# The last feed-forward's second product in seven block products for tile pairs, with its weights' conversions two at a time in the expert slots

## The chip, the cores and the metric

One core of one Trainium2 chip runs the kernel. The metric is device microseconds of one execution. The core's engines work side by side, each through its own queue in order: TensorE (PE; its weight loads are listed apart as PEld), VectorE (DVE), ScalarE (ACT), GpSimd (POOL) and SyncE (SP), which here only issues transfers.

## The reference

Attention over 4 batches, 8 heads, 576 positions of 64 gives 2304 tokens of 512. A mixture of 8 experts (top 1, hidden size 1024) follows, and a dense feed-forward of hidden size 2048. Cut to the last two:

```python
def _moe_ref(x, expert_emb, tau, w1, w2):     # x 2304x512, w1 8x512x1024, w2 8x1024x512
    ...
    for e in range(E):
        mask = expert_idx == e
        h = np.maximum(x[mask] @ w1[e], 0.0)
        out[mask] = gate_w[mask, None] * (h @ w2[e])

def _moe2_ref(x, w_in, w_out):                # w_in 512x2048, w_out 2048x512
    h = x @ w_in
    r = np.maximum(h, 0.0)
    g = r * r
    return (g @ w_out).astype(np.float32)
```

## The kernel before

Every product is made of f16 parts: an operand is split in a high and a low f16 part, and three matmuls (high x high, high x low, low x high) stand for one. The order of the instructions on each engine is that of the code; waits between engines are put in by the program's buffers.

The kernel has three stages. Attention takes the first 395 us. Then come 22 expert slots of 128 tokens each (`run_slots`). Slot t gathers its tokens with indirect transfers on POOL (`gather_id`, `gather_x`), splits them (`x_split`: ACT the high part, POOL the low part), transposes them on PE (`x_T`), multiplies by the expert's first matrix (`ff1`, 2 x 48 matmuls of 128 columns, PSUM buffer `ph`) and by its second (`ff2`, 24 matmuls of 512 columns), and stores the rows in `y_d` (`ff2_out`): the early slots in order through SP, the later ones by an indirect scatter on POOL. The loop runs ahead: in slot t stand, in this order, `gather_x(t+4)`, `ff1(t+1, 0)`, `x_T(t+2)`, `x_split(t+3)`, `ff1(t+1, 1)`, `split_w1(t+2)` and `ff2(t)` with `ff2_out(t)`. `split_w1` splits a new expert's first matrix into the single buffer `w1b` (four times ACT and DVE), behind a branch that is taken only where the expert changes, which it does in eight slots.

The feed-forward's weights `win` and `wout` arrive as 64-bit floats and are made into two f16 parts by bit operations (`convert`): four on DVE, a copy with rounding on ACT (high part), a subtraction on DVE (low part). The 16 pieces of `win` and the first 4 of `wout`, each 512 columns wide, are converted in the slots, from slot 3 on (`piece`, `CPACE` 3.3 steps to a slot, three steps to a piece); the other 12 pieces of `wout` in the first two blocks of the last stage (`PACE2`). The slots' pieces of `wout` go to DRAM (`wosc`) and come back.

The last stage takes the tokens in five blocks, four of 4 tiles (512 columns) and one of 2 (256). `g_unit(j, f)` computes one of 16 slices of the hidden layer for block j: 12 matmuls with the weights stationary and the tokens moving, relu on ACT, the square on ACT (blocks 0 and 1) or DVE, and the split, which is put off by one unit (`g_split`: ACT high part, DVE low part). `o_unit(j, n)` computes the outputs of one tile with 48 matmuls of 512 columns:

```python
for f in range(16):
    for a, b in ((0, 0), (0, 1), (1, 0)):
        PE.matmul(p_, lhsT=g2[:, a, f, n * P:(n + 1) * P], rhs=woh[:, b, f, :],
                  start=(i == 0), stop=(i == 47))
```

Its result is scaled (ACT or DVE, by tile) and scattered to the output by POOL. The block's outputs stand between the next block's `g_unit`s, one for four of them, from block 2 on; those of block 0 follow block 1's units. The next block's tokens are loaded at f = 0 (`y_load`), split in units 4 to 10 (`y_split`) and transposed by a transfer.

Of the kernel before, what the change touches and what calls it, by code (L numbers as in the profile page):

```python
# [23 lines left out]
P = 128  # L24
# [59 lines left out]
def body(ctx: ExitStack, tc: tile.TileContext, q, k, v, wsm, emb, tau, mw1, mw2, win, wout, cst_d, lsk_d, ids_d, out):  # L84
# [9 lines left out]
    wosc = dram.tile([P, 2 * 16 * DM], F16, name="wosc")  # L94
# [856 lines left out]
    with tc.manual_schedule():  # L951
# [149 lines left out]
        def convert(i, wrp, bufs, woh=None):  # L1101
            wr = wrp.tile([P, 512, 2], U32, name="wr2", bufs=bufs)
            wf = wr.rearrange("p n t -> p (n t)")
            if i < 16:
                kc, n = divmod(i, 4)
                SP.dma_start(out=wf, in_=win[kc * P:(kc + 1) * P, n * 1024:(n + 1) * 1024])
                dh, dl = (wih[:, a, kc, n * 512:(n + 1) * 512] for a in range(2))
                s = WIS
            else:
                j = i - 16  # L1110
                SP.dma_start(out=wf, in_=wout[j * P:(j + 1) * P, :])
                if woh is None:
# [14 lines left out]
            DVE.scalar_tensor_tensor(out=b, in0=hi, scalar=0xC0000000, in1=b, op0=ALU.bitwise_and, op1=ALU.bitwise_or)  # L1127
            yield
            ACT.activation(dh, bf, AF.Copy, scale=s)
            yield  # L1130
            DVE.scalar_tensor_tensor(out=dl, in0=bf, scalar=s, in1=dh, op0=ALU.mult, op1=ALU.subtract)
            if i >= 16 and woh is None:
                SP.dma_start(out=wosc.rearrange("p (a n) -> p a n", a=2)[:, :, j * 512:(j + 1) * 512], in_=wo)


        def pieces(cs, ahead):
            for c in cs[:ahead]:
                next(c)
            yield
            for n, c in enumerate(cs):  # L1140
                next(c)
                yield
                next(c)
                yield
                if n > 0:
                    next(cs[n - 1], None)
                    if n - 1 + ahead < len(cs):
                        next(cs[n - 1 + ahead])
                next(c)
                yield  # L1150
            next(cs[-1], None)
            yield

# [65 lines left out]
        def ff2_out(t):  # L1219
            ys = ysp.tile([P, XW], F32, name="ys")  # L1220
            ACT.activation(ys[:, :DM], pys.pop(t), AF.Copy, scale=YS)
            POOL.tensor_copy(ys[:, DM:XW], ga.pop(t))
            if t < NEARLY:
                SP.dma_start(out=y_d[t * P:(t + 1) * P, :], in_=ys)
            else:
                POOL.indirect_dma_start(out=y_d, out_offset=bass.IndirectOffsetOnAxis(ap=yidx[:, t:t + 1], axis=0),
                                        in_=ys, in_offset=None, bounds_check=NT + P - 1, oob_is_err=False)
# [23 lines left out]
        def piece(t, n):  # L1251
            while t >= 3 and done[0] < (t - 3 + 0.25 * n) * CPACE:
                next(conv, None)
                done[0] += 1

        def run_slots(lo, hi):
# [34 lines left out]
            for t in range(lo, hi):  # L1291
# [56 lines left out]
        with ExitStack() as fctx:  # L1348
            fp = lambda n, bufs, **kw: tp(fctx, n, bufs, **(kw if "space" in kw else dict(side="right")))
            woh = fp("f_wo", 1).tile([P, 2, 16, DM], F16, name="woh")  # L1350
            gp = fp("f_g", 2)
            yrp = fp("f_yr", 1)
            wrp2 = fp("f_wr", 1)
            ytp = fp("f_yt", 1)
            rp2 = fp("f_r", 3)
            op_ = fp("f_o", 3)
            ysp2 = fp("f_ys", 2)
            pf1 = fp("f_p1", 4, space=PSUM)
            pf2 = fp("f_p2", 4, space=PSUM)
            blocks = [list(range(i, min(i + 4, NTILE))) for i in range(0, NTILE, 4)]  # L1360
            yts, gts, yrs, late = {0: y0}, {}, {}, []

            def y_load(j):
                n, i0 = len(blocks[j]), blocks[j][0]
                yrs[j] = yrp.tile([P, 4, XW], F32, name="yr")
                SP.dma_start(out=yrs[j][:, :n], in_=y_d[i0 * P:(i0 + n) * P, :].rearrange("(n p) c -> p n c", p=P))
                yts[j] = ytp.tile([P, 2, 4, 512], F16, name="y2") if j % 2 else y0

            def y_split(j, n):
                if n >= len(blocks[j]):  # L1370
                    return
                y2, yr = yts[j], yrs[j][:, n]
                y_rows(blocks[j][n], yr)
                ysr = ysp2.tile([P, 2, 4, P], F16, name="ysr")
                y4 = yr[:, :DM].rearrange("p (k n) -> p k n", k=4)
                ACT.copy(ysr[:, 0], y4)
                DVE.tensor_tensor(out=ysr[:, 1], in0=y4, in1=ysr[:, 0], op=ALU.subtract)
                SP.dma_start_transpose(out=y2.rearrange("p a k n -> p (a k) n")[:, :, n * P:(n + 1) * P],
                                       in_=ysr.rearrange("p a k n -> p (a k n)"))

            def g_unit(j, f):
                n = len(blocks[j]) * P
                y2 = yts[j]
                if f == 0:
                    gts[j] = gp.tile([P, 2, 16, 512], F16, name="g2")
                p_ = pf1.tile([P, 512], F32, name="pf1")
                i = 0
                for kc in range(4):
                    for a, b in ((0, 0), (0, 1), (1, 0)):
                        PE.matmul(p_[:, :n], lhsT=wih[:, a, kc, f * P:(f + 1) * P], rhs=y2[:, b, kc, :n],  # L1390
                                  start=(i == 0), stop=(i == 11))
                        i += 1
                r = rp2.tile([P, 512], F32, name="r")
                ACT.activation(r[:, :n], p_[:, :n], AF.Relu, scale=RS)  # L1394
                g = rp2.tile([P, 512], F32, name="g")
# [124 lines left out]
```

## Time and profile before

| | us |
|---|---|
| median of three runs | 1032.59 (1025.32 to 1034.40) |
| the profiled execution | 1032.91 |
| its span in the trace | 1031.1 |
| attention, to about | 395 |
| expert slots, to about | 643 |
| last feed-forward on PE | 643.16 to 1019.79 |

The span runs from the first instruction to the last, so 1.8 us of the profiled execution lie outside it. A timeline row gives start, duration, engine, line, operation, buffers and shape of neighbouring instructions that belong together, with their count, and in brackets the idle time ahead of the first and what ended it. Neighbouring groups of PE overlap by a matmul's run through the array, so the spacing of two starts tells what a group costs. A group's row gives busy time and the mean of one instruction in ns.

### The profile page before, as it was taken

The numbers are of one execution on the slowest core, as the hardware profiler recorded it, in microseconds if no ns is written. First come the engines' busy times: TensorE is split into PE (matmuls) and PEld (weight loads), VectorE is DVE, ScalarE is ACT, GpSimd is POOL, SyncE is SP. The second block draws the span as 40 slices with busy tenths as digits, with TensorE's granted clock in tenths as the row PEclk, the third lists the DMA queues.
The fourth block names the chain that finished last, engine by engine and source line by source line (L and its number), as shares of the span: only waits on it lengthen the run. The fifth ranks groups of instructions, "written<-read, shape, count | busy, mean of one in ns | idle before, by whom it ended". The sixth has DMA issues, their size and how long they took to land. (4 is left out here: it accounts for less than half of the span.)

```text
span 1031.1 us, 21983 instructions
## 1 busy us (share of the span) xinstructions
PE 966.3 (94%) x8309; PEld 610.9 (59%) x8309; DVE 589.2 (57%) x1338; ACT 507.6 (49%) x1058; POOL 281.6 (27%) x261
## 2 busy tenths in 40 slices
PE   8687999999899889999989999999999999999995
PEld 4355676677577767776767775444444444445652
DVE  6665899888989774657785635577403322331210
ACT  5575677767877573455565532667402311321210
POOL 1212537446533353353646331000010000000000
PEclk9798999999999899999999999999999999999998
DMA  8989885988789333399988532553300110100000
GB/s 293 303 225 287 282 285 196 288 245 284 231 261 319 124 124 125 122 328 372 322 325 312 167 95 73 184 154 82 92 21 27 41 35 11 42 11 11 22 21 20
DMA packets 79583, 174.39 MB, mean 169 GB/s; under 512 B 26120, under 2 KB 27272, under 8 KB 78928
## 3 DMA queue, kind: packets, MB, share of 16 engines
q1 hardware_dynamic: 73408, 157.39, 47.2%
q0 software_dynamic: 6064, 15.54, 4.5%
q8 instruction: 67, 1.10, 0.4%
q14 instruction: 44, 0.36, 0.1%
HBM read 165.36 MB, written 45.43 MB: 204 GB/s over the span
## 5 line engine op out<-in xcount | busy, mean ns | idle before, releaser
L1416 PE MATMUL pf<-woh,g 128*128 128x512 f16 x864 | 188.6, 379 | 0.0
L1390 PEld LDWEIGHTS <-wih 128*128 128x128 f16 x960 | 93.8, 98 | 98.3 <-issue 5.3
L1416 PEld LDWEIGHTS <-g 128*128 128x128 f16 x864 | 84.5, 98 | 101.1
L1198 PE MATMUL ph<-x,w1b 128*128 128x128 f16 x2112 | 125.1, 219 | 1.9 <-ACTq L1024 0.7
L1198 PEld LDWEIGHTS <-w1b 128*128 128x128 f16 x2112 | 120.5, 98 | 6.1 <-ACTq L1024 0.9
L1213 PE MATMUL py<-vt,h 128*128 128x512 f16 x528 | 117.8, 379 | 1.1 <-DMA vt<-wsc 1.0
L522 ACT ACTIVATE pr<-ssb,mn 128x576 f32<-128x576 f32 x144 | 111.7, 776 | 12.9 <-DVE mn L509 12.8
L1422 POOL DMA_INDIRECT out_dram<-o,orow x18 | 17.7, 985 | 358.1 <-DVE o L1421 222.4
L509 DVE CUSTOM_DVE_ANT_0 ssb<-ps_s,bias 128x576 f32<-128x576 f32 x144 | 107.4, 748 | 7.2 <-DMA bias<-bias_d 4.8
L498 PE MATMUL ps_s<-kst,qd 128*128 128x288 f16 (+1 forms) x640 | 97.4, 293 | 12.0 <-DVE mn L509 8.9
L1390 PE MATMUL pf<-big,wih 128*128 128x512 f16 (+1 forms) x576 | 105.3, 344 | 1.0 <-PEq L1342 1.0
L1394 ACT ACTIVATE r<-pf 128x512 f32<-128x512 f32 (+1 forms) x80 | 44.1, 551 | 123.4 <-PE pf L1390 123.4
L471 POOL TENSOR_TENSOR wh<-wr,w2s_c 128x1024 f16<-128x1024 f32 x32 | 61.8, 1930 | 133.3 <-DMA wr<-in_mw_dram 62.8
L531 PE MATMUL ps_t<-cst,pr 128*128 128x128 f32 x576 | 94.1, 287 | 0.9 <-DVE pt L209 0.6
L1399 DVE TENSOR_TENSOR g<-r 128x512 f32<-128x512 f32 (+1 forms) x48 | 29.0, 603 | 114.6 <-ACT r L1394 114.5
L1390 PE MATMUL pf<-y,wih 128*128 128x512 f16 x384 | 84.0, 379 | 2.8 <-ACT r L1394 2.2
L1213 PEld LDWEIGHTS <-h 128*128 128x128 f16 x528 | 50.8, 98 | 59.0 <-issue 2.0
L556 PE MATMUL pv<-pt,vt 128*64 128x128 f32 (+1 forms) x1280 | 84.5, 276 | 0.0
L531 PEld LDWEIGHTS ps_t<-cst,pr 128*128 128x128 f32 x576 | 66.3, 147 | 24.3 <-issue 19.1
L556 PEld LDWEIGHTS pv<-pt,vt 128*64 128x64 f32 x1280 | 66.2, 141 | 12.7 <-issue 11.6
L498 PEld LDWEIGHTS <-qd 128*128 128x128 f16 (+1 forms) x640 | 57.0, 102 | 27.4 <-issue 17.2
L1204 DVE SCALAR_TENSOR_TENSOR h<-ph,h 128x512 f16<-128x512 f32 x44 | 30.3, 690 | 71.2 <-ACT h L1203 44.8
(190 smaller groups left out, 1379.6 us busy)
## 6 DMA issues: line engine op xcount, KB each, us to landing
vt<-wsc SPq DMA_DIRECT2D x88, 512.0 KB
wr<-in_mw_dram SPq DMA_DIRECT2D x76, 512.0 KB
kst<-in_mw_dram SPq DMA_DIRECT2D x44, 512.0 KB
wsc<-wh SPq DMA_DIRECT2D x32, 512.0 KB
bias<-bias_d SPq DMA_DIRECT2D x16, 576.0 KB
bias_d<-rt SPq DMA_DIRECT2D x28, 295.5 KB
qd<-qh SPq DMA_DIRECT2D x64, 128.0 KB
wr<-in_win_dram SPq DMA_DIRECT2D x16, 512.0 KB
```

The source lines that it names most:

```text
L471: POOL.tensor_tensor(out=wh[:, 0], in0=wr, in1=w2s_c.to_broadcast([P, 1024]), op=ALU.mult)
L498: PE.matmul(s[r, hf, :288], lhsT=qd[:, h2, i, pr, r], rhs=kst[x - x % 2][:, pr, h2, x % 2, js], start=(i == 0), stop=(i == 1))
L509: DVE.tensor_tensor_reduce(out=ss.rearrange("p (a j) -> p a j", a=2), in0=s[:, :, :288], in1=btile[bkey[u]][:, h2].rearrange("p (a j) -> p ...
L522: ACT.activation(pr_sb[k_ // 2][:, h2], ssb.pop(k_), AF.Exp, bias=mns.pop(k_), scale=-1.0, accum_out=sums[c, b][:, h:h + 1])
L531: PE.transpose(pt_ps[k_][:, jc * P:(jc + 1) * P], src[:, j0:j0 + P], eye)
L556: PE.matmul(pv[o, cs], lhsT=vb[:, 2 * jc + h2, d] if jc < 4 else vb[o, 8, d], rhs=a[h2][:, jc, cs] if jc < 4 else e[o, cs], start=(jc == 4 ...
L1198: PE.matmul(p_[:, f4, :], lhsT=w[:, a, kc, f * P:(f + 1) * P], rhs=x2[:, b, kc, :], start=(i == 0), stop=(i == 11))
L1204: DVE.scalar_tensor_tensor(out=h2[:, 1, o], in0=p_, scalar=0.0, in1=h2[:, 0, o], op0=ALU.max, op1=ALU.subtract)
L1213: PE.matmul(p_, lhsT=h2[:, a, fc, :], rhs=wb2[fc // 2][:, b, fc % 2, :], start=(i == 0), stop=(i == 23))
L1390: PE.matmul(p_[:, :n], lhsT=wih[:, a, kc, f * P:(f + 1) * P], rhs=y2[:, b, kc, :n], start=(i == 0), stop=(i == 11))
L1394: ACT.activation(r[:, :n], p_[:, :n], AF.Relu, scale=RS)
L1416: PE.matmul(p_, lhsT=g2[:, a, f, n * P:(n + 1) * P], rhs=woh[:, b, f, :], start=(i == 0), stop=(i == 47))
```

## The change

The last stage's tokens are taken in nine pairs of tiles (256 columns). The hidden layer's two halves (f and f + 8) and the pair's two tiles make a 2 x 2 arrangement of blocks, and the second product is computed with seven block products in place of eight, in the way of Strassen and Winograd: four sums of blocks on the hidden side (POOL, `g_unit`), four on the weights' side (POOL, `convert`), and sums of the products partly in PSUM (four banks, `pa` to `pd`) and partly by `comb` on DVE. The matmuls of the last stage before were 960 in the first product (768 of 512 columns, 192 of 256) and 864 of 512 columns in the second; now there are 1728 and 9 x 7 x 24 = 1512, all of 256 columns. A product of the pair before stands ahead of each `g_unit` from c = 3 on (c = 5 in block 1), and what is left of the seven behind the block. The low parts are made for two c at a time, for seven blocks in one instruction.

All weights are converted in the slots: 8 pieces of `win` and 8 of `wout`, 1024 columns wide, two pieces under way at a time (`pieces`, `CPACE` 6.1 steps to a slot, seven steps to a piece, from slot 2 on, with the first loads in slot 0). Clearing the sign moves from DVE to ACT (`Abs`). A `wout` piece gets its four sums on POOL and is stored to `wosc` with 128 x 3584 f16 elements; the last stage begins with eight loads of as much back into `woh`.

A slot's store of its outputs is put off: `ff2_out` keeps it, and `y_out` issues it in the next slot behind `x_split`. The copy of the gates (`ys<-ga`) moves from POOL to DVE. The tokens' splits use the four buffers `us_t`, and each tile takes two transposing transfers in place of one. The host lays `wout` out in another order of rows and columns.

On DVE, in a late expert slot with a new expert, this stood there (`h` is the low part of ff1's result, `w1b` the expert's matrix, `wb` and `wr` a piece in conversion, `us` tokens of the last stage):

```order
L1204 SCALAR_TENSOR_TENSOR h_9054<-ph,h_9054 128x512 x2
L1024 COMPARE_AND_BRANCH
L1015 SCALAR_TENSOR_TENSOR w1b<-kst_103,w1b 128x2x512 x4
L1024 UNCONDITIONAL_BRANCH x2
L1019 TENSOR_LOAD ne_i
L1131 SCALAR_TENSOR_TENSOR wih<-wb,wih 128x512
L1122 TENSOR_SCALAR wb<-wr_8745 128x512
L1123 TENSOR_SCALAR wb<-wb 128x512
L1124 TENSOR_SCALAR wb<-wb 128x512
L1125 SCALAR_TENSOR_TENSOR wb<-wr_8745,wb 128x512
L1127 SCALAR_TENSOR_TENSOR wb<-wr_8745,wb 128x512
```

and stands now (`tb` and `wr` are pieces in conversion):

```order
L1123 SCALAR_TENSOR_TENSOR tb<-wr_8001,tb 128x1024
L1244 COPY ys<-ga 128x2
L1118 TENSOR_SCALAR tb<-tb 128x1024
L1119 TENSOR_SCALAR tb<-tb 128x1024
L1038 TENSOR_TENSOR xs<-us_76,xs 128x512
L1260 COPY meta<-us_76 128x2
L1261 CAST orow<-us_76 128x1
L1226 SCALAR_TENSOR_TENSOR h_9043<-ph,h_9043 128x512
L1121 SCALAR_TENSOR_TENSOR tb<-wr_8307,tb 128x1024
L1142 SCALAR_TENSOR_TENSOR wr_8001<-tb,wr_8001 128x1792
L1226 SCALAR_TENSOR_TENSOR h_9043<-ph,h_9043 128x512
L1024 COMPARE_AND_BRANCH
```

One piece of 512 columns per slot has become most of a piece of 1024, the operations of two pieces alternate, the gates' copy has come in, and two of them stand between the two halves of `h`, ahead of the branch with the split of `w1b`.

On POOL, in the late slots, before (`xg` and `xs` are a slot's tokens and their low part, `ti` the indices):

```order
L987 DMA xg<-x_d,ti 128x515
L1037 TENSOR_SCALAR xg<-xg 128x512
L1038 TENSOR_TENSOR xs<-xg,xs 128x512
L1045 COPY ga<-xg 128x2
L1222 COPY ys<-ga 128x2
L1024 UNCONDITIONAL_BRANCH
L1226 DMA y_d<-ys,yidx 2432x514
L977 DMA ti<-id_d,xidx 128x1
```

and now:

```order
L1136 TENSOR_TENSOR tb<-tb 128x256 x4
L987 DMA xg<-x_d,ti 128x515
L1037 TENSOR_SCALAR xg<-xg 128x512
L1038 TENSOR_TENSOR xs<-xg,xs 128x512
L1045 COPY ga<-xg 128x2
L1253 DMA y_d<-ys,yidx 2432x514
```

The scatter to `y_d` at that place is now the one of the slot before, behind the split of the tokens and not ahead of the next gather; four sums for a piece of `wout` have come in ahead of the gather, and the copy to `ys` is gone.

On DVE, in the last stage, before (`ysr` tokens, `g` the hidden layer, `o` the outputs):

```order
L1233 COPY meta<-yr 128x2
L1234 CAST orow<-yr 128x1
L1377 TENSOR_TENSOR ysr<-yr,ysr 128x512
L1399 TENSOR_TENSOR g<-r 128x512
L1407 TENSOR_TENSOR g_12360<-g,g_12360 128x512
L1421 TENSOR_SCALAR o<-pf_12722,meta 128x512
```

and now (`u` is an intermediate sum of the products, `gf` the squared blocks):

```order
L1463 SCALAR_TENSOR_TENSOR u_14546<-pf_c,meta,u_14491 128x256
L1433 TENSOR_TENSOR gf<-gf 128x1024
L1444 TENSOR_TENSOR g_14303<-gf,g_14303 128x7x256
L1260 COPY meta<-us_76 128x2
L1261 CAST orow<-us_76 128x1
L1407 TENSOR_TENSOR ysr<-us_76,ysr 128x512
L1463 SCALAR_TENSOR_TENSOR o_14397<-pf_d,meta,u_14546 128x256
```

The subtraction that makes the low parts covers seven blocks of 256 at a time, and the sums of the products stand between the squares and these.

The diff, cut to its core:

```diff
 def convert
...
+            ACT.activation(bf, hi.bitcast(F32), AF.Abs)
+            yield
             DVE.tensor_scalar(bf, bf, TINY64, None, op0=ALU.max)
             DVE.tensor_scalar(b, b, 3, 0x3FFFFFF8, op0=ALU.logical_shift_left, op1=ALU.bitwise_and)
...
+            for d, x, y, op in ((4, 0, 1, ALU.subtract), (5, 2, 4, ALU.subtract), (6, 2, 0, ALU.subtract),
+                                (7, 3, 5, ALU.subtract)):
+                POOL.tensor_tensor(out=tb[:, d], in0=tb[:, x], in1=tb[:, y], op=op)
             yield
...
+            ACT.activation(dh, flat[:, 256:], AF.Copy, scale=WOS)
+            yield
+            DVE.scalar_tensor_tensor(out=dl, in0=flat[:, 256:], scalar=WOS, in1=dh, op0=ALU.mult, op1=ALU.subtract)
+            yield
+            SP.dma_start(out=wosc[:, g * 3584:(g + 1) * 3584], in_=wo)
...
 def ff2_out
-            POOL.tensor_copy(ys[:, DM:XW], ga.pop(t))
...
+            DVE.tensor_copy(ys[:, DM:XW], ga.pop(t))
+            yd.append((t, ys))
...
 def piece
-            while t >= 3 and done[0] < (t - 3 + 0.25 * n) * CPACE:
+            while done[0] < (1 if t < 2 else 1 + (t - 2 + 0.25 * n) * CPACE):
...
 in run_slots
                 if live(3):
                     x_split(t + 3)
+                y_out()
...
 in the last stage
-            def g_unit(j, f):
...
+            def g_unit(j, c):
...
+                ACT.activation(g[:, 0:4, c % 2, :], p_.rearrange("p h (i n) -> p (h i) n", i=2), AF.Relu, scale=RS)
+                if c % 2 == 0:
+                    return
+                g4 = g[:, 0:4].rearrange("p q c n -> p (q c n)")
                 if j < 2:
+                    ACT.activation(g4, g4, AF.Square)
                 else:
+                    DVE.tensor_tensor(out=g4, in0=g4, in1=g4, op=ALU.mult)
+                for d, x, y, op in ((4, 0, 2, ALU.add), (5, 4, 1, ALU.subtract), (6, 1, 0, ALU.subtract),
+                                    (7, 3, 5, ALU.subtract)):
+                    POOL.tensor_tensor(out=g[:, d], in0=g[:, x], in1=g[:, y], op=op)
                 g_split()
+                late.append((g, gts[j], c - 1))
...
+                    ACT.copy(gt[:, 0, :, c:c + 2, :], g[:, 1:8])
+                    DVE.tensor_tensor(out=gt[:, 1, :, c:c + 2, :], in0=g[:, 1:8], in1=gt[:, 0, :, c:c + 2, :], op=ALU.subtract)
...
+            def ff2_of(j):
...
+                def prod(ps, s, w, first, end):
+                    i = 0
+                    for c in range(8):
+                        for a, b in ((0, 0), (0, 1), (1, 0)):
+                            PE.matmul(ps, lhsT=gt[:, a, s, c, :], rhs=woh[:, c, b, w, :],
+                                      start=(i == 0 and first), stop=(i == 23 and end), skip_group_check=True)
+                            i += 1
...
+                prod(pa, 0, 0, True, False)
+                s = [u(f"s{i}") for i in range(2)]
+                for i in range(2):
+                    ACT.activation(s[i], pa, AF.Copy, scale=m[i])
+                yield
+                prod(pb, 4, 4, True, True)
+                u2 = [u(f"u{i}") for i in range(2)]
+                for i in range(2):
+                    comb(u2[i], pb, i, s[i])
+                yield
...
+            for g in range(8):
+                SP.dma_start(out=woh[:, g].rearrange("p a q n -> p (a q n)"), in_=wosc[:, g * 3584:(g + 1) * 3584])
+            for j in range(NB):
+                two = ff2_of(j - 1) if j else iter(())
+                last = j == NB - 1
+                for c in range(8):
+                    if c > (2 if j > 1 else 4) and not (last and c == 6):
+                        next(two, None)
+                    g_unit(j, c)
...
+                if last:
                     g_split()
+                for _ in two:
+                    pass
+            for _ in ff2_of(NB - 1):
+                pass
```

## Rows read from the trace of the kernel before

**Rows 1.** The page, part 1: engine, busy us, share, instructions.

```profile
PE 966.3 (94%) x8309; PEld 610.9 (59%) x8309; DVE 589.2 (57%) x1338; ACT 507.6 (49%) x1058; POOL 281.6 (27%) x261
```

**Rows 2.** Waits of PE, 480 to 1031: what waited, releaser: us, times, longest.

```profile
PE px L1181 <- POOL xs L1038: 2.6, 1, 2.6
PE pf L1390 <- ACT r L1394: 2.2, 2, 1.8
PE pf L1390 <- PEq L1342: 1.0, 1, 1.0
...
PE pf L1390 <- DMA y<-ysr: 0.6, 1, 0.6
```

**Rows 3.** Timeline of PE, 915 to 1031: start, duration, line, operation, count.

```profile
926.15 10.52 PE L1416 MATMUL pf<-woh,g 128*128 128x512 f16 x48
936.51 5.40 PE L1390 MATMUL pf<-big,wih 128*128 128x256 f16 x48
941.75 10.52 PE L1416 MATMUL pf<-woh,g 128*128 128x512 f16 x48
...
988.55 31.24 PE L1416 MATMUL pf<-woh,g 128*128 128x512 f16 x144
```

**Rows 4.** Timeline of PE, 395 to 660.

```profile
489.16 2.84 PE L1198 MATMUL ph<-x,w1b 128*128 128x128 f16 x48
491.84 0.61 PE L1181 MATMUL px<-eye,xs 128*128 128x128 f16 x8
...
494.97 5.34 PE L1213 MATMUL py<-vt,h 128*128 128x512 f16 x24
500.15 2.84 PE L1198 MATMUL ph<-x,w1b 128*128 128x128 f16 x48
...
539.45 0.40 PE L1181 MATMUL px<-eye,xs 128*128 128x128 f16 x4 [2.64 <-POOL xs L1038]
...
643.16 17.21 PE L1390 MATMUL pf<-big,wih 128*128 128x512 f16 x79 [1.05 <-PEq L1342]
```

**Rows 5.** Windows of 5 and 25 us: busy time by engine, clock, DMA share, GB/s.

```profile
655.00:660.00 5.00, 5.00 (x25) 2.25 (x24) 3.10 (x7) 4.48 (x9) 0.00 (x0) 1.00 1.02 378
...
900.00:925.00 25.00, 25.00 (x117) 11.37 (x116) 7.77 (x12) 6.63 (x12) 0.99 (x1) 1.00 0.03 11
```

**Rows 6.** Groups by line and form, 643 to 1031: busy us, mean ns, idle before.

```profile
L1390 PEld LDWEIGHTS <-wih 128*128 128x128 f16 x960 | 93.8, 98 | 98.3 <-issue 5.3
...
L1407 DVE TENSOR_TENSOR g<-g,g 128x512 f16<-128x512 f32 x64 | 43.8, 686 | 10.8 <-ACT g L1406 10.7
L1406 ACT CAST g<-g 128x512 f16<-128x512 f32 x64 | 38.7, 606 | 0.0
...
L1406 ACT CAST g<-g 128x256 f16<-128x256 f32 x16 | 6.3, 396 | 0.0
...
L1123 DVE TENSOR_SCALAR wb<-wb 128x512 f32<-128x512 f32 x12 | 5.1, 428 | 0.4
```

**Rows 7.** The page, part 5: a POOL group of the attention stage.

```profile
L471 POOL TENSOR_TENSOR wh<-wr,w2s_c 128x1024 f16<-128x1024 f32 x32 | 61.8, 1930 | 133.3 <-DMA wr<-in_mw_dram 62.8
```

**Rows 8.** Groups by line and form of POOL, 450 to 500.

```profile
L1038 POOL TENSOR_TENSOR xs<-xg,xs 128x512 f16<-128x512 f32 x5 | 6.1, 1220 | 0.4
```

**Rows 9.** The same of DVE.

```profile
L1015 DVE SCALAR_TENSOR_TENSOR w1b<-kst,w1b 128x1024 f16<-128x1024 f32 x8 | 9.3, 1220 | 0.5 <-ACT w1b L1014 0.5
```

**Rows 10.** Timeline of POOL, 528 to 550.

```profile
531.57 2.10 POOL L1226 DMA_INDIRECT y_d<-ys,yidx  x1 [12.67 <-ACT w1b L1014]
...
545.48 1.70 POOL L1038 TENSOR_TENSOR xs<-xg,xs 128x512 f16<-128x512 f32 x1
```

**Rows 11.** Timeline of DVE, 535 to 550.

```profile
535.49 0.68 DVE L1131 SCALAR_TENSOR_TENSOR wih<-wb,wih 128x512 f16<-128x512 f32 x1
...
546.08 1.65 DVE L1131 SCALAR_TENSOR_TENSOR wih<-wb,wih 128x512 f16<-128x512 f32 x1
```

**Rows 12.** Records of L1342 (pools closed): duration min/median/max, first and last start.

```profile
L1342 POOLq INC_SWDGE_SEM  x1: 1896/1896/1896, 650.5 to 650.5; - x1
```

More of the change, by code (lines that the diff above doesn't have):

```diff
@@ L1128, in convert @@
             yield
-            ACT.activation(dh, bf, AF.Copy, scale=s)
-            yield
[L1131 to L1137, printed above, removed]
+            if i < NWIN:
+                yield
+                dh, dl = (wih[:, a, kc, n * 1024:(n + 1) * 1024] for a in range(2))
+                ACT.activation(dh, af, AF.Copy, scale=WIS)
+                yield
+                DVE.scalar_tensor_tensor(out=dl, in0=af, scalar=WIS, in1=dh, op0=ALU.mult, op1=ALU.subtract)
+                yield
+                return
@@ L1138, in pieces @@
+            yield
+            SP.dma_start(out=wosc[:, g * 3584:(g + 1) * 3584], in_=wo)
+        def pieces(cs):
+            for c in cs[:4]:
                 next(c)
             yield
-            for n, c in enumerate(cs):
-                next(c)
+            next(cs[0])
+            yield
+            none = iter(())
+            for n in range(len(cs) + 1):
+                c, d = cs[n] if n < len(cs) else none, cs[n - 1] if n else none
+                next(c, None)
+                if 0 < n <= NWIN and n + 3 < len(cs):
+                    next(cs[n + 3])
@@ L1303, in run_slots @@
                     ff1(t + 1, 0)
+                if first:
+                    piece(t, 0)
                 if live(2):
@@ L1319, in run_slots @@
                     more(t)
+                    piece(t, 2)
                     piece(t, 3)
@@ L1338, in body @@
         run_slots(0, NMOST)
+        y_out()
         for _ in conv:
@@ L1357, in body @@
+            up = fp("f_u", 1)
             ysp2 = fp("f_ys", 2)
             pf1 = fp("f_p1", 4, space=PSUM)
-            pf2 = fp("f_p2", 4, space=PSUM)
-            blocks = [list(range(i, min(i + 4, NTILE))) for i in range(0, NTILE, 4)]
-            yts, gts, yrs, late = {0: y0}, {}, {}, []
+            pf2 = fp("f_p2", 1, space=PSUM)
+            NB = NTILE // 2
+            gts, gfs, late = {}, {}, []
+            yv = lambda j: y0[:, :, :, 256 * (j % 2):256 * (j % 2) + 256]
             def y_load(j):
[L1364 to L1367, printed above, removed]
@@ L1375, in y_split @@
                 y4 = yr[:, :DM].rearrange("p (k n) -> p k n", k=4)
+                o = slice(t % 2 * P, t % 2 * P + P)
                 ACT.copy(ysr[:, 0], y4)
                 DVE.tensor_tensor(out=ysr[:, 1], in0=y4, in1=ysr[:, 0], op=ALU.subtract)
-                SP.dma_start_transpose(out=y2.rearrange("p a k n -> p (a k) n")[:, :, n * P:(n + 1) * P],
-                                       in_=ysr.rearrange("p a k n -> p (a k n)"))
-            def g_unit(j, f):
[L1382 to L1395, printed above, removed]
```

211 lines of the change are left out of this document (111 added, 100 removed).

## The prediction

> **What bounds the kernel now.** The page's first part comes first: PE is busy for 966.3 us of a span of 1031.1 [rows 1], so a change counts by what PE executes and by what it waits for. The list of PE's waits from 480 us on is next: four waits, 6.4 us together [rows 2]. So from there to the end PE works nearly without a break, and the last feed-forward is bound by PE's own time. It begins at 643.16 [rows 4]; its last group begins at 988.55 and takes 31.24 [rows 3], so PE is done at 1019.8: 376.6 us. In a window of that stage PE is busy 25.00 of 25 us at a granted clock of 1.00, the 2.4 GHz level, with DVE at 7.77, ACT at 6.63 and POOL at 0.99 [rows 5]. The other engines are two thirds idle there, and the clock has nothing left to give.
>
> The price of a matmul comes from the spacing of group starts in the timeline. 48 matmuls of 512 columns take 936.51 - 926.15 = 10.36 us, 215.8 ns each; 48 of 256 columns take 941.75 - 936.51 = 5.24 us, 109.2 ns each [rows 3]; 48 of 128 columns take 491.84 - 489.16 = 2.68 us, 56 ns each [rows 4]. Price follows columns, and a matmul of half the columns costs 1.3 ns more than half.
>
> **The last feed-forward, PE's work.** Before: (768 + 864) x 215.8 ns + 192 x 109.2 ns = 352.2 + 21.0 = 373.2 us, and 3.8 us of the waits of [rows 2] (2.2, 1.0, 0.6), together 377.0 against 376.6 measured, so the prices hold. After: 1728 + 1512 = 3240 matmuls at 109.2 = 353.8 us. In columns the second product falls to seven eighths, 442,368 to 387,072. That is 55,296 columns or 23.3 us less, and the halving of 1632 matmuls takes 3.9 us of it back.
>
> The Trainium skill, page "TensorE: Matmul & The Clock Gate", section "Back-to-back issue gap", speaks against this: it gives a sustained spacing of about 131 ns at 512 columns and 81 ns at 128, where weight loads and matmuls overlap. By a straight line between, an estimate for 256 is 98 ns, the stage before would be 233 us and the stage after 317 us, so the change would lose 84 us. The trace has 215.8, 109.2 and 56 ns at these sizes, and by the rows above the measurement decides.
>
> **What the other engines must deliver in time.** No group of before has the new sizes, so I interpolate. An ACT cast takes 396 ns at 256 and 606 at 512 elements [rows 6], 0.82 ns per element, so 1.03 us at 1024 and 1.66 at 1792. A DVE subtraction takes 686 ns at 512 [rows 6], a like operation 1220 at 1024 [rows 9], so about 2.0 us at 1792. A sum on POOL takes 1220 ns at 512 [rows 8] and 1930 at 1024 [rows 7], so 0.87 at 256 and 3.5 for four. For two c PE takes 48 matmuls, 5.24 us (10.5 with two products between); the other engines need for them ACT two relus, perhaps a square, and a cast (2.9 to 3.9), POOL 3.5, DVE 2.0 and perhaps a square of 1.2. None is near the bound, so only latencies count.
>
> First, **the low parts of a pair's last two c.** They are put off to behind c = 1 of the next block. There c = 1 ends 5.24 us into the block; relu and cast follow (0.25 to start, 0.6, 1.66), to 7.75; the subtraction ends at 9.8. From block 2 on the first product begins behind c = 2, at 7.86, and needs these low parts at its 20th matmul, at 10.05. So 0.3 us are to spare, if nothing holds DVE. But POOL is at the next sums then, and [rows 11] show a DVE operation of 0.68 take 1.65 us beside a POOL sum that itself took 1.70 [rows 10]. One such hit adds 1.0 and PE waits 0.7. I take half, 0.35 x 7 blocks = 2.4 us (0 to 4.9).
>
> Second, **the start.** POOL, free early in the stage before, now works for it. At the close of the slots' pools it is held until 650.5 + 1.9 = 652.4 [rows 12], and the first sums wait for that. Block 0's four lots of sums then end near 652.4 + 14 = 666.4, the last low parts some 4 us later; the first product of block 0 stands at 643.2 + 13 x 2.62 = 677.2. PE has four buffers of `pf1` ahead of the late sums; I take 0.5 us (0 to 3).
>
> Third, **the weights' return.** Eight loads, 7.34 MB, wait for the same clearing, 652.4. At 378 GB/s, what the queues moved at that place before [rows 5], they take 19.4 us, to 672; block 0's first product needs the last eighth at about 679.5. Hidden, with 7 us to spare. Half that rate would be late by 11.7.
>
> Fourth, **the end.** Behind the last unit three products (7.9 us) cover the last relu, square, sums, cast and subtraction (0.25 + 0.6 + 1.2 + 3.5 + 1.66 + 2.0 = 9.2, needed at 10.0): 0.5 us (0 to 1.5). The wait for transposed tokens of 0.6 [rows 2] stays. The wait of 2.2 for ACT stood beside the conversions, which are gone.
>
> The stage: 353.8 + 2.4 + 0.5 + 0.5 + 0.6 = 357.8 us, 18.8 less than 376.6.
>
> **The expert slots.** They are bound by PE as well: a slot takes 500.15 - 489.16 = 10.99 us [rows 4]. DVE: a 512-column operation with one operand takes 428 ns [rows 6], so at most 0.86 at 1024. A piece of `win` is two of these and three of 1220 [rows 9], 5.4 us, of `wout` 6.2; at 6.1 / 7 = 0.87 pieces a slot that is 4.7 to 5.4. A slot with a new expert adds 4 x 1.22 for `w1b`, 1.4 for `h` and some small ones: 11 to 11.7 us of 10.99. Eight slots of 22 have that and the others only some 7, so DVE falls behind by under a microsecond and recovers. Its place on the path is the low part of `w1b` ahead of the next `ff1`: 5.18 us of `ff2` cover [rows 4], and 0.69 + 2 x 1.22 stand behind the piece's two operations (up to 3.2 us, begun some 3 us before): about 1.2 us to spare. Interleaving two pieces keeps DVE from waiting on ACT or POOL for its own piece. POOL gets 3.5 us per `wout` piece, 3.0 of a slot's 10.99.
>
> The one stall of PE there, 2.64 us at 539.45 [rows 4], comes from POOL: a scatter of `ys` sat at its head, idle 12.67 before it [rows 10], with the next gather and split behind it. Now the split goes ahead of the scatter, so this goes: -2.6. What comes in: more DVE and POOL operations at once (hits as in [rows 11]), and bigger loads and stores among the experts'. Nothing prices it; between 0 and +6 I take +1.6, since PE is fed a slot ahead. Slots: -1.0.
>
> **The sum.** From the profiled execution's own 1032.9 (0.3 above the median): 1032.9 - 18.8 - 1.0 = 1013 us.
>
> **The rivals.**
> *A, no latency shows.* DVE is not hit and the slots take the load for nothing: -3.4 in the last stage, -1.6 in the slots, 1008. For it: 0.3 us to spare on paper, and the first `L1131` of [rows 11] kept its 0.68. Against: by my prices POOL is at sums just while the subtraction runs.
> *B, the weights come late.* At half the rate of [rows 5] PE stands for 11.7 us, once: 1024. For it: the rate is from one window with other transfers. Against: 27.1 us are there for 7.34 MB, so PE waits only below 271 GB/s.
> *C, DVE is hit twice per block.* The subtraction takes 4 us in place of 2, PE waits 1.7 x 7 = 11.6, that is 9.2 more: 1022. For it: the subtraction is as long as two sums. Against: the one hit that the rows show cost 1.0.
> *D, the slots lose.* A late split, sum or transfer costs 0.3 us in each of 20 slots: 6 in place of 1.6, 1018. For it: a slot with a new expert asks more of DVE than it lasts. Against: only eight of them do.
> *E, slower: short matmuls cost more than half.* A weight load takes 98 ns [rows 6]; now there are 3240 where 1824 were. If a load no longer hid behind a stream of 256 columns, each matmul would grow. The saving is gone at (376.6 - 4.0 + 1.0) / 3240 = 115 ns, and the kernel is slower by 1% from 118 ns on; with the load fully added, 98 + 109 ns, it takes 3240 x 98 ns = 318 us more, 1331. Against: 109.2 and 56 ns, with the same loads [rows 3, 4]. The Trainium skill, page "TensorE: Matmul & The Clock Gate", section "Back-to-back issue gap", gives a loss too, near 1117 us by the estimate above; the trace's 215.8 ns where it has 131 leave it no chance beyond that of E.
>
> **How the numbers follow.** My forecast has 0.37, A 0.25, D 0.15, C 0.12, B 0.07, E 0.02, a mixture of others 0.02. Predicted: 1013. The range goes from below A (1005) to C (1022), leaving out B, E and some of the tails. A measurement of this kernel tells about 1% from no change, here 1022.3 and 1042.9. "Same" gets B, some of C and the tail of D: 0.10; "slower" E and a little: 0.03; "faster" 0.87.
>
> **What would show it.** Right: the last stage's groups of 24 and 48 matmuls spaced by 2.62 and 5.24 us; about 358 us from its first matmul to its last; waits of PE before the first product of blocks 2 to 8 of under 0.7 us, released by the subtraction (`g`, L1444); no wait for POOL in the slots. Wrong: a spacing over 115 ns; one long wait for `woh`; repeated waits over 1 us for DVE; slots longer than 11 us.

## The result, and the profile after

The changed kernel takes 1018.61 us in the median, before it 1030.88: a ratio of 0.9885, 95% interval 0.9856 to 0.9914. It is faster by a little over 1%. The ratios here and below leave out the executions that ran over 1.5% longer than the fastest of their kernel, which the medians keep (without them the changed kernel has 1017.9, e3 1023.5 and e9 1020.9 us). The profiled execution took 1020.09 us, its span is 1018.3; 12.8 us less than in the profile before.

Four stretches of the two traces show where these 12.8 us come from. The changed code begins to matter at slot 0, whose `ff2` is the first group of PE on the line of `ff2`; ahead of it stand only the first four loads of pieces.

| stretch | before | after | difference |
|---|---|---|---|
| up to the first `ff2` (attention, same code) | 406.0 | 402.4 | -3.6 |
| first `ff2` to the last feed-forward | 237.1 | 248.5 | +11.3 |
| last feed-forward on PE | 376.6 | 354.9 | -21.7 |
| from there to the end of the span | 11.3 | 12.5 | +1.2 |

The first line is no effect of the change: in the twelve profiles of this study, all of kernels with the same attention, the first `ff2` begins anywhere from 398.8 to 408.5 us. So the change gains 20.5 us at the end and gives back 11.3 in the expert slots: 9.2 us in all.

The last stage, in the timeline of PE of the changed kernel (columns as in [rows 3]):

```profile
650.91 34.22 PE L1420 MATMUL pf<-big,wih 128*128 128x256 f16 x312 [1.54 <-PEq L1374]
684.97 2.78 PE L1458 MATMUL pf_a<-woh,g 128*128 128x256 f16 x24
...
719.03 2.79 PE L1458 MATMUL pf_a<-woh,g 128*128 128x256 f16 x24
721.66 2.78 PE L1420 MATMUL pf<-big,wih 128*128 128x256 f16 x24
...
987.31 2.78 PE L1458 MATMUL pf_a<-woh,g 128*128 128x256 f16 x24 [0.82 <-ACT o L1488]
...
1003.03 2.78 PE L1458 MATMUL pf_d<-woh,g 128*128 128x256 f16 x24
```

It begins at 650.91 and ends at 1003.03 + 2.78 = 1005.8. Between 719.03 and 721.66 lie 24 matmuls of 256 columns: 2.63 us, within 0.01 of the price of [rows 3]. 3240 x 109.2 ns are 353.8 us, so all waits and seams of the stage make 1.1 us. The only wait that the trace names is 0.82 ahead of the last pair's first product. In windows (busy time of PE, PEld, DVE, ACT, POOL, then clock, DMA share and GB/s) the stage looks so, beside the place in the slots where most time went at once:

```profile
670.00:675.00 5.00, 5.00 (x48) 4.49 (x47) 2.57 (x1) 2.31 (x3) 4.41 (x4) 1.00 1.01 417
...
900.00:925.00 25.00, 25.00 (x232) 22.32 (x230) 11.00 (x8) 9.54 (x12) 12.90 (x12) 1.00 0.15 47
480.00:485.00 5.00, 3.12 (x10) 1.22 (x10) 4.58 (x5) 3.92 (x5) 4.46 (x5) 0.77 1.03 417
```

At 900 us DVE is busy for 11.00 of 25 us and POOL for 12.90, where [rows 5] had 7.77 and 0.99; PE is full all the same, at the 2.4 GHz level. The weights come back at 417 to 423 GB/s and are there at about 678.

The waits of PE from 400 us on, in the slots and the last stage (columns as in [rows 2]):

```profile
PE py L1235 <- DMA vt<-wsc: 3.8, 3, 2.4
PE ph L1220 <- DVEq L1024: 2.6, 2, 2.1
PE ph L1220 <- DVE w1b L1015: 1.8, 2, 1.2
PE ph L1220 <- ACTq L1024: 1.6, 2, 1.4
...
PE pf_a L1458 <- ACT o L1488: 0.8, 1, 0.8
PE px L1203 <- POOL xs L1038: 0.3, 1, 0.3
```

The 2.6 us for POOL of [rows 2] are 0.3 now. In their place stand 3.8 us for the experts' second matrices (`vt` from `wsc`; 1.0 before) and 6.0 us for DVE and ACT at the branch and split of `w1b`. The matmuls behind the long ones run slower too:

```profile
481.88 7.03 PE L1235 MATMUL py<-vt,h 128*128 128x512 f16 x24 [2.38 <-DMA vt<-wsc]
...
560.82 4.37 PE L1220 MATMUL ph<-x,w1b 128*128 128x128 f16 x46 [2.11 <-DVEq L1024]
...
575.26 0.51 PE L1220 MATMUL ph<-x,w1b 128*128 128x128 f16 x6 [1.21 <-DVE w1b L1015]
```

As rows, 24 matmuls of 512 columns last 5.34 us at full clock and 7.03 here; 46 of 128 last 2.74 elsewhere and 4.37 here. The granted clock is 0.77 in the window from 480 to 485 us, and 0.66 from 560 to 565. Of the 11.3 us about 7 are longer waits between the first `ff2` and the last stage (4.7 us before, 11.7 now, with the 1.54 at its entry), and about 3 these slower matmuls.

### The profile page after: what moved, and what is told of

It is laid out like the page before. It is cut to its first block, busy times and chain, and to the rows that moved or that the text cites. A ratio compares the mean times of both kernels' runs of the same rounds, so it can differ in the third digit from the quotient of the medians.

```text
span 1018.3 us, 24810 instructions
## 1 busy us (share of the span) xinstructions
PE 946.7 (93%) x9725; PEld 747.8 (73%) x9725; DVE 662.0 (65%) x1229; ACT 540.9 (53%) x1000; POOL 499.1 (49%) x415
## 5 line engine op out<-in xcount | busy, mean ns | idle before, releaser
L1436 POOL TENSOR_TENSOR gf<-gf 128x256 f32<-128x256 f32 x144 | 166.0, 1172 | 131.0 <-DVE gf L1433 108.8
L1420 PE MATMUL pf<-big,wih 128*128 128x256 f16 x1728 | 196.0, 273 | 1.5 <-PEq L1374 1.5
L1420 PEld LDWEIGHTS <-wih 128*128 128x128 f16 x1728 | 169.0, 98 | 21.6 <-issue 2.0
L1458 PEld LDWEIGHTS <-g 128*128 128x128 f16 x1512 | 147.4, 98 | 18.7 <-issue 1.0
L1426 ACT ACTIVATE gf<-pf 128x512 f32<-128x512 f32 x72 | 42.5, 597 | 193.3 <-PE pf L1420 140.3
L1220 PE MATMUL ph<-x,w1b 128*128 128x128 f16 x2112 | 127.5, 220 | 7.9 <-DVEq L1024 3.0
L1444 DVE TENSOR_TENSOR g<-gf,g 128x1792 f16<-128x1792 f32 x36 | 85.5, 2374 | 50.1 <-ACT g L1443 50.1
L1433 DVE TENSOR_TENSOR gf<-gf 128x1024 f32<-128x1024 f32 x28 | 34.3, 1226 | 113.6 <-ACT gf L1426 113.6
L498 PE MATMUL ps_s<-kst,qd 128*128 128x288 f16 (+1 forms) x640 | 96.6, 292 | 11.7 <-DVE mn L509 9.2
L556 PEld LDWEIGHTS pv<-pt,vt 128*64 128x64 f32 x1280 | 65.5, 140 | 12.5 <-issue 11.4
L1443 ACT CAST g<-gf 128x1792 f16<-128x1792 f32 x36 | 60.3, 1676 | 4.4 <-POOL gf L1436 4.4
```

Source lines behind the costliest of these rows:

```text
L498: PE.matmul(s[r, hf, :288], lhsT=qd[:, h2, i, pr, r], rhs=kst[x - x % 2][:, pr, h2, x % 2, js], start=(i == 0), stop=(i == 1))
L556: PE.matmul(pv[o, cs], lhsT=vb[:, 2 * jc + h2, d] if jc < 4 else vb[o, 8, d], rhs=a[h2][:, jc, cs] if jc < 4 else e[o, cs], start=(jc == 4 ...
L1220: PE.matmul(p_[:, f4, :], lhsT=w[:, a, kc, f * P:(f + 1) * P], rhs=x2[:, b, kc, :], start=(i == 0), stop=(i == 11))
L1420: PE.matmul(p_[:, h], lhsT=wih[:, a, kc, f * P:(f + 1) * P], rhs=y2[:, b, kc, :], start=(i == 0), stop=(i == 11))
L1436: POOL.tensor_tensor(out=g[:, d], in0=g[:, x], in1=g[:, y], op=op)
L1444: DVE.tensor_tensor(out=gt[:, 1, :, c:c + 2, :], in0=g[:, 1:8], in1=gt[:, 0, :, c:c + 2, :], op=ALU.subtract)
```

## The experiments

The two causes in question stand in the trace of the changed kernel. **Transfers:** pieces of 1 MB go into the same queue as the experts' weights. **Sums:** ACT executes in order, and its rounding of a `wout` piece waits for POOL. The timelines of ACT, POOL and DVE from 545 to 595 us show the second:

```profile
552.70 1.70 ACT L1140 ACTIVATE wr<-tb 128x1792 f16<-128x1792 f32 x1 [5.77 <-POOL tb L1136]
...
568.87 1.70 ACT L1140 ACTIVATE wr<-tb 128x1792 f16<-128x1792 f32 x1 [3.05 <-POOL tb L1136]
...
585.10 1.70 ACT L1140 ACTIVATE wr<-tb 128x1792 f16<-128x1792 f32 x1 [1.39 <-POOL tb L1136]
```

```profile
546.26 1.16 POOL L1038 TENSOR_TENSOR xs<-xg,xs 128x512 f16<-128x512 f32 x1
...
548.25 1.48 POOL L1253 DMA_INDIRECT y_d<-ys,yidx  x1 [0.17 <-DVE tb L1118]
549.75 2.91 POOL L1136 TENSOR_TENSOR tb<-tb 128x256 f32<-128x256 f32 x4
```

```profile
554.99 0.69 DVE L1038 TENSOR_TENSOR xs<-us,xs 128x512 f16<-128x512 f32 x1 [6.23 <-ACT xs L1034]
...
560.02 0.68 DVE L1226 SCALAR_TENSOR_TENSOR h<-ph,h 128x512 f16<-128x512 f32 x1
```

POOL splits tokens, issues the scatter and then begins the sums at 549.75. ACT stands 5.77 us for them, and behind it in its queue are the split `xs` of a tile for the last stage and the relu `h`. DVE stands 6.23 us for `xs`. So the second half of `h` comes only at 560.02, and PE, which waits for DVE to pass the branch, stands 2.11 us.

**e1, the sums on DVE.**

```diff
-                POOL.tensor_tensor(out=tb[:, d], in0=tb[:, x], in1=tb[:, y], op=op)
+                DVE.tensor_tensor(out=tb[:, d], in0=tb[:, x], in1=tb[:, y], op=op)
```

> The changed kernel with one edit: the four sums of a wout piece run on DVE in place of POOL. In the changed kernel's trace the expert slots, from the first ff2 to the last feed-forward, last 248.5 us against 237.2 before, and PE waits there behind ACT and DVE from 555 us on. Theory 'sums': ACT, in order, stands at the rounding of a wout piece until POOL's sums are done, and what is queued behind it is late; then this kernel loses none of the 5 to 7 us between 555 and 590, and its slots take about 242 us, the whole about 1012. Theory 'DVE': DVE itself is the engine that is late, by its bigger pieces; then 1.7 us more of DVE per piece make the slots longer than 248.5, the whole 1020 or more. Theory 'transfers': only the waits for the experts' weights count; then the slots stay within 2 us of 248.5.

It takes 1012.63 us, ratio 0.9843 (0.9823 to 0.9863). Slots 239.9 us, last stage as in the changed kernel. All waits of PE from 400 us on:

```profile
PE py L1235 <- DMA vt<-wsc: 4.5, 2, 2.7
PE pf L1420 <- PEq L1374: 1.8, 1, 1.8
PE pf_a L1458 <- ACT o L1488: 0.8, 1, 0.8
```

The waits for DVE and ACT are gone, although DVE has 1.8 us more to do for each piece (four sums of 447 ns). So DVE's load was not the cause of them; that ACT stood for POOL, or that POOL worked beside DVE, was.

**e2, 12 of the 16 piece loads left out.** The later pieces convert what lies in the first four buffers.

```diff
...
-                SP.dma_start(out=wf, in_=win[kc * P:(kc + 1) * P, n * 2048:(n + 1) * 2048])
+                if i < 4:
+                    SP.dma_start(out=wf, in_=win[kc * P:(kc + 1) * P, n * 2048:(n + 1) * 2048])
...
-                SP.dma_start(out=wf, in_=wout[g * P:(g + 1) * P, :])
...
```

> The changed kernel with 12 of the 16 loads of conversion pieces left out (the first four loads stay, later pieces convert what lies there, so the output is not the reference's); all conversions, sums and stores stay. Theory 'transfers': PE's waits for the experts' weights (vt from wsc, 3.8 us, with 1.7 us of matmuls at a lower clock behind them) come from 1 MB loads queued among the experts' transfers; they go, and the slots take about 243 us in place of 248.5. Theory 'sums' or 'DVE': the waits from 555 us on stay, and they alone make 6 us or more of the 11.3. If transfers cause both, the slots fall to 238.

Slots 243.7 us, and no wait for `vt` in the list; the waits for DVE and ACT at `w1b` stay (5.6 us). One of 1.84 us for `xs` from POOL comes in at 606. The whole time, 1015.5 (0.9881, 0.9843 to 0.9919), does not tell it from the changed kernel, with attention as uneven as it is; the trace does.

**e5, both.** The edits of e1 and e2 together.

> The changed kernel with the sums of wout on DVE and 12 of the 16 piece loads left out (so the output is not the reference's). Apart, the sums on DVE took the slots from 248.5 to 239.9 us, the missing loads to 243.7. If the two causes are separate (ACT standing at POOL's sums; the experts' weights late behind piece loads), both together give 234 to 236 us, and PE waits in the slots for less than 1 us in all. If they are one chain, the slots stay near 239.

1002.38 us, ratio 0.9744 (0.967 to 0.9818), slots 233.5 us. All waits of PE from 399 us on:

```profile
PE pf L1424 <- PEq L1378: 1.5, 1, 1.5
PE pf_a L1462 <- ACT o L1492: 0.8, 1, 0.8
```

Not one wait in the slots but that at the entry of the last stage. 8.6 and 4.8 us apart, 15.0 together: two separate causes, and more than the 11.3 lost, as the kernel before has waits of its own there.

**e3, the scatter back at its place.**

```diff
                 ff2_out(t)
+                y_out()
```

> The changed kernel with the scatter of a slot's outputs issued right behind ff2_out again, as before, and not in the next slot behind the token split. The prediction gave this move 2.6 us, by the one stall of 2.64 us at 539 us. If that holds, the stall of PE for xs comes back, 2 to 3 us, and the slots take about 251 us. If the scatter's new place itself delays the sums of wout (it stands ahead of them on POOL), the slots are shorter than 248.5.

Slots 248.3 us, as without the edit; PE stands 1.39 us for `xs`, against 0.34 in the changed kernel and 2.64 before. The whole, 1024.84 (0.9936, 0.9909 to 0.9963), is above the changed kernel's, yet its trace has the first `ff2` at 408.5, so 6 us of it lie ahead of the edit. That the move makes the slots shorter isn't shown, nor that it is what took the stall away. In the changed kernel a scatter still sits at POOL's head at this place, with the next gather and split behind it:

```profile
530.89 1.08 POOL L1253 DMA_INDIRECT y_d<-ys,yidx  x1 [10.98 <-DMA wr<-in_mw_dram]
```

```profile
538.03 0.40 PE L1203 MATMUL px<-eye,xs 128*128 128x128 f16 x4 [0.34 <-POOL xs L1038]
```

Counted from the first `ff2`, it starts 128.5 us in, later than before (125.6), and the split is done at 135.6 (133.4 before). But PE comes to these transposes at 134.9 in place of 130.4, since it has waited for `vt` by then. In e3 it comes at 133.3, and in e9, which keeps the move, at 132.0 and stands 2.08 us.

**e4, the first product one unit earlier.**

```diff
-                    if c > (2 if j > 1 else 4) and not (last and c == 6):
+                    if c > (1 if j > 1 else 4) and not (last and c == 6):
```

> The changed kernel with the first block product of a pair one unit earlier, ahead of c = 2 and not of c = 3, in blocks 2 to 8. By the prediction's latencies the low parts of the last two c then are ready 0.3 us before the point that is now 2.6 us later, so PE would wait about 2.3 us per block, 16 us in all. If the chain is faster than worked out, the wait is shorter: it measures the slack that the changed kernel has, 2.6 us less the wait. Theory that there is plenty of slack: under 0.5 us per block.

One execution, 1043.46 us. Waits of PE from 700 us on and the first of them in the timeline:

```profile
PE pf_a L1458 <- DVE g L1444: 15.6, 8, 2.0
PE pf_a L1458 <- ACT g L1443: 3.2, 8, 1.1
```

```profile
712.64 2.13 PE L1458 MATMUL pf_a<-woh,g 128*128 128x256 f16 x18
715.07 0.39 PE L1458 MATMUL pf_a<-woh,g 128*128 128x256 f16 x2 [0.30 <-ACT g L1443]
717.44 0.61 PE L1458 MATMUL pf_a<-woh,g 128*128 128x256 f16 x4 [1.98 <-DVE g L1444]
717.89 4.45 PE L1420 MATMUL pf<-big,wih 128*128 128x256 f16 x24
722.18 2.78 PE L1458 MATMUL pf_b<-woh,g 128*128 128x256 f16 x24
```

PE idles 0.30 us for the rounding and 1.98 for the subtraction, 2.28 together. What the product loses is more, since groups no longer overlap across a wait, and is read from the starts: 20 matmuls at 109.2 ns are 2.18 us, but the 21st starts 717.44 - 712.64 = 4.80 behind the first. That is 2.62 us late, all that the product was moved by. So in the changed kernel it has nothing to spare, within 0.02 us. The stage is 27.1 us longer: seven times 2.62, another 6.7 since behind four of the seven waits, alike in length, 24 matmuls last 4.45 us in place of 2.78, and the rest at the last pair's first product, where an eighth wait (2.76 us in place of 0.82) stands.

**e6, the rounding later, sums on POOL.**

```diff
 in pieces
                 next(c, None)
                 if 0 < n <= NWIN and n + 3 < len(cs):
                     next(cs[n + 3])
                 yield
-                next(d, None)
                 yield
...
                 next(c, None)
+                next(d, None)
                 yield
```

> The changed kernel with its sums on POOL as they are; only ACT's rounding of a piece stands two steps (a third of a slot, 3.6 us) later in the program's order, and DVE's low part one step later. Theory 'queue': ACT stands in order at the rounding until POOL, behind its gathers, token split and scatter, has made the sums (5.8, 3.1 and 1.4 us at 552, 568 and 585); then most of these waits go, and the slots take 241 to 245 us in place of 248.5. Theory 'port': POOL's sums hold up DVE by running beside it, whatever waits for them; then the slots stay within 2 us of 248.5.

1012.66 us, ratio 0.9831 (0.9768 to 0.9895), slots 244.2. ACT's waits for the sums from 540 to 600 fall from 10.2 us to 1.9, PE's waits for DVE and ACT at `w1b` from 6.0 to 2.6. With POOL's work the same as in the changed kernel, the later rounding gives back about 4 of the 8.6 us of e1 (DVE's low part of a piece stands one step later too, so it is not ACT's order alone). What of the rest is the place of the sums in POOL's queue and what is POOL slowing DVE stays open.

**e7, the conversions from slot 1; e8, two paces.** Both with the edit of e1:

```diff
-            while done[0] < (1 if t < 2 else 1 + (t - 2 + 0.25 * n) * CPACE):
+            while done[0] < (1 if t < 1 else 1 + (t - 1 + 0.25 * n) * CPACE):
```

```diff
-            while done[0] < (1 if t < 2 else 1 + (t - 2 + 0.25 * n) * CPACE):
+            while done[0] < (1 if t < 2 else 1 + min(t - 2 + 0.25 * n, 10) * 4.5 + max(t - 12 + 0.25 * n, 0) * 7.6):
```

> A version meant to be better than both kernels: sums of wout on DVE, and the conversions begin in slot 1 instead of slot 2 (the first four loads stay in slot 0), so that loads go out earlier, where the queues have room (0.2 of their share from 415 to 425 us). If that takes load out of the two places where PE waits for the experts' weights (480 and 516 us, 4.5 us with sums on DVE), slots of 236 to 239 us; if it only shifts the same loads, 240 as with the sums on DVE alone; if DVE is too busy in slot 1, more than 240.

> A version meant to be better than both kernels: sums of wout on DVE, and two paces in place of one, 4.5 steps a slot up to slot 12 and 7.6 from there, since the queues are full from 475 to 530 us and half empty from 555 on. If the experts' weights come late because of the sum of bytes in that stretch, a quarter fewer piece loads there (0.64 a slot in place of 0.87) take away most of the 4.5 us of waits: slots of 235 to 238 us. If it is not the sum but single loads that happen to stand ahead, 240. If DVE can't carry more than a piece a slot with the sums (8 us of 11), the late slots grow and it takes 242 or more.

e7: 1016.25 us (0.9848, 0.9767 to 0.9929), slots 242.6, waits for `vt` still 4.4. Beginning earlier only shifts the loads, and 2.4 us of waits for DVE come in at 454 and 551 us. e8: 1009.41 us, ratio 0.9756 (0.9712 to 0.98), slots 238.1 us. Waits of PE from 400 us on:

```profile
PE py L1235 <- DMA vt<-wsc: 2.4, 2, 1.6
PE ph L1220 <- DVEq L1024: 1.8, 3, 1.1
PE pf L1420 <- PEq L1374: 1.5, 1, 1.5
...
PE ph L1220 <- ACTq L1024: 0.7, 1, 0.7
PE px L1203 <- POOL xs L1038: 0.3, 1, 0.3
```

A quarter fewer loads up to slot 12 halve the waits for `vt`, 4.5 to 2.4 us; 2.5 us for DVE and ACT come in. This version is the fastest here that computes everything, 2.4% below the kernel before; in its slots it is only 1.8 us below e1.

**e9, two paces with sums on POOL** (the edits of e6 and of e8's pace), and **e10, the changed kernel once more** beside them:

> The same two paces with the sums on POOL and the rounding two steps later, where one pace gave slots of 244.2 us with 4.8 us of waits for the experts' weights and 3 us for DVE. Fewer loads up to slot 12: under 2 us of such waits, 240 to 241. If POOL is the limit with more pieces in the late slots (3 to 4.3 us of sums for each), waits for DVE or ACT grow by 2 us or more and the slots stay at 244.

> The changed kernel as it is, beside the two versions on the same chip. Slots of 246 to 251 us and a last stage of 355 us from its first matmul to its last; if the slots' waits come and go with the execution, fewer than 245 or more than 252.

e9: 1022.78 us (0.9865, 0.9807 to 0.9923), slots 249.9. The waits for `vt` fall to 2.6 as in e8, but one of 4.6 us for ACT and one of 2.2 for DVE come in behind slot 14. From 560 to 650 us ACT stands 13.0 us for the sums on POOL; POOL itself idles ahead of several of these sums for DVE, so that it is the limit isn't shown. The first units of the last stage wait 2.4 us for ACT too. e10: 1019.98 us (0.987, 0.982 to 0.9919), slots 251.3, with 5.6 us of waits for `vt` and 7.7 for DVE, ACT and POOL. So the loss in the slots is there in each profile of this kernel. The 1.82 us for POOL stand at 614, where four sums (3.81 us from 605.37) go ahead of the token split. Together with e4, three profiles of the same slots have 248.2, 248.5 and 251.3 us: 3 us between executions. The 8.6 of e1 and the 15.0 of e5 stand clear of that. For the 4.8 of e2, the 4.3 of e6 and the 1.8 between e1 and e8 the waits that go are the better evidence.

## Why the prediction was right or wrong

The time, 1018.6, lies in the range, 5.6 us above the value. Two terms missed in opposite directions, the slots by 12.3 us and the last stage by 2.9. That the time is in the range is in part luck: the profiled execution had 3.6 us less ahead of the changed code, and 1032.9 less the 9.2 that the change is worth is 1023.7, above the range's 1022.

**The price of a matmul held.** 109.2 ns at 256 columns over 3240 matmuls, 353.8 us on paper, 354.9 with all waits. Rival E is out. (The halved matmuls are 768 + 756 = 1524 and not 1632; the 3.9 us that they take back hold.) The sustained 131 ns at 512 columns of the Trainium skill, page "TensorE: Matmul & The Clock Gate", section "Back-to-back issue gap", does not show here: the trace has 215.8 ns before and 109.2 at 256 columns now, where the estimate from that page was 98.

**The latencies of the last stage were counted too dear.** Of 4.0 us (2.4 + 0.5 + 0.5 + 0.6) the trace has 0.8, at the end. The step that failed is "I take half, 0.35 x 7 blocks". The chain was right, and the subtraction was hit, but by a third of what was taken, as these groups of the stage show (columns as in [rows 6]):

```profile
L1436 POOL TENSOR_TENSOR gf<-gf 128x256 f32<-128x256 f32 x144 | 166.0, 1172 | 131.0 <-DVE gf L1433 108.8 <-ACT gf L1431 19.5
...
L1444 DVE TENSOR_TENSOR g<-gf,g 128x1792 f16<-128x1792 f32 x36 | 85.5, 2374 | 50.1 <-ACT g L1443 50.1
L1443 ACT CAST g<-gf 128x1792 f16<-128x1792 f32 x36 | 60.3, 1676 | 4.4 <-POOL gf L1436 4.4
...
L1260 DVE COPY meta<-us 128x2 f32<-128x2 f32 x14 | 9.6, 686 | 0.0
```

2374 ns in the mean against an estimate of 2.0 us, and 1676 against 1.66 for ACT. At the point in question:

```profile
717.11 1.68 ACT L1443 CAST g<-gf 128x1792 f16<-128x1792 f32 x1
```

```profile
718.82 2.34 DVE L1444 TENSOR_TENSOR g<-gf,g 128x1792 f16<-128x1792 f32 x1 [0.35 <-ACT g L1443]
```

With POOL's sums beside it the subtraction takes 2.34 us; the stage's last one, with POOL idle, takes 2.03. So a hit costs 0.3 us and not 1.0. It ends at 721.16, and the product that began at 719.03 needs it at its 21st matmul, behind 20, at 719.03 + 20 x 0.1092 = 721.21. The 0.3 us to spare on paper are used up: in all seven blocks this product lasts 2.79 us in place of 2.78, and e4 finds nothing left. That no wait shows is as much luck as margin. Rival A has the outcome right and not its reason, as DVE is hit in each block. Rival C is out (its 1.7 x 7 would be 11.9 and not 11.6). A sum on POOL of 256 elements takes 1172 ns in this stage, a third more than the 0.87 that I interpolated. Inside the stage PE does not wait for it, but the 0.82 us at the end come from there: ACT stands 4.36 us for the last sums, and the copy that frees `pf_a` (L1488) stands behind that cast in its queue. The prediction's fourth term priced the low parts there and not this bank; its 0.5 us was near by size alone.

**The start and the weights' return** held: no wait, the return done at 678 for a product at 684.97. Rival B is out.

**The tail** after PE grew by 1.2 us, which I had left out.

**The slots are the term that was wrong:** +11.3 in place of -1.0. Rival D came nearest, but its 6 us less the 2.6 for the scatter would have been +3.4, spread over 20 slots; the trace has the loss in five places, around 480, 518, 560, 575 and 589. That its 1018 meets the time is chance. Four sentences of the prediction failed. "POOL gets 3.5 us per `wout` piece, 3.0 of a slot's 10.99" weighed POOL's time and not its queue: the sums stand behind the token split and the scatter. "Interleaving two pieces keeps DVE from waiting on ACT or POOL for its own piece" left out what else DVE waits for: ACT stands for the sums, everything in order behind it is late, and DVE stands 6.23 us for `xs`. e1 gives 8.6 us for this, together with what POOL's sums may do to DVE beside them; e6 gives about 4 for the later rounding. And "+1.6" for larger loads was too little: e2 gives 4.8 us. The stretch from 435 to 530 us was near the queues' limit already: a new expert takes 4 MB in a slot of 11 us, in the kernel before the queues' share stood at 1.02 from 475 to 480 and from 510 to 515, and PE waited 1.0 us for `vt`:

```profile
475.00:480.00 5.00, 5.00 (x63) 3.82 (x62) 3.42 (x6) 1.23 (x2) 3.05 (x5) 1.00 1.02 409
510.00:515.00 5.00, 5.00 (x77) 4.36 (x75) 4.30 (x9) 2.04 (x4) 1.85 (x2) 1.00 1.02 407
```

```profile
PE py L1213 <- DMA vt<-wsc: 1.0, 2, 0.6
```

The fourth is "Now the split goes ahead of the scatter, so this goes: -2.6". The stall fell from 2.64 to 0.34, but not by this: at that place the scatter is still ahead, and PE came 4.5 us later. DVE falling behind by its own work in slots with a new expert, on which I spent most working, was no cause: e1 loads it more and has no wait for it.

## What to carry to other kernels

Work that is moved from a stage with idle engines into one that PE bounds is not free because the engines' busy shares have room. For each moved step ask which in-order queue it stands in, what it waits for there, and what stands behind it. A sum on an engine with a long queue is dear when another engine must wait for it in order; the same sum on a busier engine, in order with its user's neighbours, brought no wait of PE here. The queue of the transfers has a margin of its own per stretch: with fewer loads where its share is full and more behind slot 12, the waits for weights halved. And a stall that is gone may have gone because PE came later: look at both sides of the wait before a move is credited with it.

## What the runs showed of the hardware

A wait of 2.0 to 2.7 us on PE can cost nearly twice as much, when the granted clock is lower behind it. In e4 the windows at and behind the first such wait show

```profile
716.00:718.00 2.00, 0.56 (x5) 0.50 (x6) 1.38 (x1) 0.00 (x0) 2.00 (x2) 0.99 0.00 0
718.00:720.00 2.00, 2.00 (x12) 1.38 (x10) 0.00 (x0) 0.84 (x2) 1.33 (x2) 0.50 0.00 0
720.00:722.00 2.00, 2.00 (x14) 1.50 (x13) 0.00 (x0) 0.00 (x0) 0.00 (x0) 0.65 0.00 0
722.00:724.00 2.00, 2.00 (x21) 1.80 (x19) 0.00 (x0) 0.60 (x1) 0.00 (x0) 1.00 0.00 0
```

0.50, the 1.2 GHz level, and then full clock again; 24 matmuls pay 1.67 us. Of seven waits alike in length only four were followed by it, the 2.68 us of e1 was, but the 2.64 us of [rows 4] before and 3.03 us in e10 were not, so the length of the wait alone does not settle it.

A small DVE operation with POOL at work beside it can take four times as long: the copy of 128 x 2 elements to `meta` takes 686 ns in the last stage (`L1260` above), where it took 161 before:

```profile
L1233 DVE COPY meta<-yr 128x2 f32<-128x2 f32 x14 | 2.3, 161 | 0.0
```

Sums of POOL ran beside all 14 of these copies. Not every operation is hit: the cast of 128 x 1 elements behind each, beside the same sums, takes 141 ns (146 before).
